# A rational feed-forward after channel attention: cubic and denominator as shifted squares, one way of splitting for every pair, and a branch to the old formulas

## The chip, the cores and the metric

The kernel runs on one core of one Trainium2 chip. The core has TensorE (PE, matmuls; PEld is its weight load), VectorE (DVE), ScalarE (ACT), GpSimd (POOL), SyncE (SP, which issues most DMAs) and 16 DMA engines. The metric is the time of one execution on the device in microseconds; before the change it is 2591.35 (median of 3 runs, 2590.48 to 2592.93). Lower is better.

## The reference

There are 4 batches of 6080 tokens with 256 channels. Attention is over channels: q and k are normalised over the tokens, their 256 x 256 product is put through a softmax, and v is multiplied by it. The result goes through a feed-forward of width 2048 whose activation is a rational function with drawn coefficients a (4) and b (2).

```
qn = q / (norm(q, over tokens) + 1e-6);  kn the same
att = softmax(kn^T @ qn / tau);  x = v @ att          # per batch, 6080 x 256
h = x @ w_in                                          # w_in 256 x 2048 (8 bytes an element)
P = a0 + a1 h + a2 h^2 + a3 h^3
Q = 1 + |b0| |h| + |b1| h^2
out = (P / (Q + 1e-6)) @ w_out                        # w_out 2048 x 256 (8 bytes an element)
```

The inputs are float32, apart from w_in and w_out.

## The kernel before, in words

**Tiling.** The attention matrix of a batch is multiplied into w_in first ("fuse": per pair two tiles w and w2, a high and a low part in float32r). So per group of 512 tokens (the twelfth of a batch has 448) the kernel forms h = v @ w directly, two blocks of 128 hidden units ("a pair") at a time: 8 pairs a group, 12 groups a batch, 384 pairs in all. v is turned on DVE and split into vhi (ACT) and vlo (POOL), both float32r.

**A pair** (function `pair`, lines 824 to 1020): PE makes hx, 128 x 2 x 512 in PSUM, with 12 float32r matmuls (vhi w, vlo w, vhi w2). ACT, DVE and POOL then turn it into g, and PE adds g @ w_out to the accumulator acc (2 banks of PSUM, one buffer). `KIND`, line 52, has four letters for each of the 8 pairs. The first says how g meets w_out: R splits g into gh and gl (both float32r), and PE does 12 float32r matmuls (gh w_out_hi, gh w_out_lo, gl w_out_hi); S keeps g in float32 (in a uu tile), and PE does 4 float32 matmuls with w_out_sb. Four pairs are R, four are S. The second letter says how the denominator is made: F and f by Abs(b1 h), times h plus b0 on DVE, Abs, and plus one (on POOL for F, on ACT for f); U by a square and an Abs on ACT and a product and a sum on POOL. The numerator is always a line a3 h + a2 on ACT ("slope") and two passes on DVE ("num1", "num2"). The reciprocal is Abs_reciprocal_sqrt ("root") and Square on ACT, then one step of correction: "quot" (DVE), "again" (POOL, two halves), "rest" (DVE) and, for R, "last_pool" (POOL), for S "last" (DVE).

**Attention.** Every batch's q and k come in 24 halves of a group into kq tiles; PE adds up their products, ACT squares them, and the squares are added on POOL, on DVE or by an adding DMA. The first batch's halves, 8 pieces of w_in and some of w_out fill the start; the first 10 halves of the second batch ("front") follow.

**Order.** Every step is handed to a `Planner` (lines 120 to 279) with a key: the due time of its pair plus an offset from the table `LAG` (by step name and pair). The planner lists the steps in the order in which a model of the engines would start them, and each engine runs its list in that order. Buffers are rings: three hx, three d, five uu, three r, three gh, two gl, one acc. Line 69 is the helper that issues every instruction, so every row of the profile has that line; rows are told apart by their tiles.

Of the kernel before, what the change touches and what calls it, by code (L numbers as in the profile page):

```python
# [20 lines left out]
LAG = {  # L21
    "first": (-24.0827, 3.1318, 94.51, -24.5032, 22.4371, -51.7071, -86.5307, -21.2765),
    "second": (32.5259, 24.2026, -35.044, 23.3497, 19.1846, -23.3758, 75.5728, 69.5328),
    "line": (-60.3793, -61.2691, -59.8342, -215.9253, -53.1915, -76.184, -176.4998, -1.9601),
    "prod": (-44.6411, -87.224, -31.8158, -156.7696, -54.2751, -78.1687, -52.424, -29.3868),
    "abs": (-34.4285, -122.1588, -58.7602, -98.9991, -109.4362, -197.9928, -178.3656, -100.9785),
    "one": (166.6146, 7.0144, 53.5865, 60.2777, 89.1595, 21.5861, 288.9329, 196.6758),
    "slope": (129.0614, 42.8295, 37.2315, 42.0834, 87.1801, 67.56, 67.4098, -36.9932),
    "num1": (215.3215, 137.6246, 221.5767, 236.6176, 228.2938, 156.502, 166.2629, 171.3395),
    "num2": (153.2124, 60.9084, 12.211, 101.4315, 108.3821, -26.7673, 155.735, 50.8239),  # L30
    "sum": (-114.3088, 29.3047, -115.4251, -167.6125, -59.476, -188.0768, -152.5494, -79.9865),
    "root": (-38.5091, -197.9471, -59.4045, -115.0584, -58.0609, -128.1065, -80.6201, -193.5267),
    "square": (-40.0553, -16.2375, -33.3815, -133.7437, 15.9887, -1.4662, -98.6254, -36.906),
    "quot": (29.4947, -54.9999, -50.3625, -122.0889, -68.6879, -40.3178, -160.6082, -31.8443),
    "again": (-51.7758, -60.2965, -172.0824, -144.6242, -186.8217, -194.2782, -221.1473, -198.5867),
    "rest": (-207.6066, -117.3149, -46.4453, -162.483, -66.4698, -127.5935, -141.4566, -70.1941),
    "last": (-85.0694, -95.1459, 38.415, -140.8617, -144.4619, -72.3023, -75.0525, -34.9464),
    "last_pool": (103.2607, 109.5359, 210.7027, 11.2587, 121.6879, -15.2807, 139.5789, 81.5984),
    "out": (172.8342, 198.8616, 134.7569, 148.4694, 113.0415, 59.72, 9.9512, 73.2606),
    "out_lo": (147.9861, 210.6514, 208.9647, 323.6963, 308.8599, 174.7979, 147.3652, 281.023),  # L40
}
# [241 lines left out]
def tile_channel_attention_rational_ffn(  # L283
# [858 lines left out]
```

## Time and profile before

| | |
|---|---|
| median of the runs | 2591.35 us |
| profiled execution: span | 2590.5 us |
| mean granted clock of TensorE | 0.993 |
| PE busy | 2500.2 us |
| DVE busy | 2379.6 us |
| POOL busy | 2318.0 us |
| ACT busy | 2260.3 us |
| DMA moved | 140.97 MB |

The profiled execution's time is its span, 2590.5 us; the median of the timed runs is 0.9 us above it. Busy times are of one engine; the matmuls of PE are pipelined, so the durations of single matmul records overlap, and the distance between their starts is what one costs. Durations of ACT and DVE records also overlap a little with the next on the same engine.

### The profile page before, as it was taken

To read this page: it belongs to the slowest core of one execution; us is meant where nothing else is said; L and a number is where in the kernel's file an instruction comes from. 1 tells how busy PE (TensorE), PEld (TensorE's weight loads), DVE (VectorE), ACT (ScalarE), POOL (GpSimd) and SP (SyncE) were. 2 spreads that over 40 slices of the span, in tenths; PEclk is the share of its full clock that TensorE was granted. 3 is DMA by queue.
4 is the path that set the end of the run, shared out by engine and by line. 5 is a ranking of instruction groups with operands and counts; after the bars stand their busy time and mean duration, and the time that the engine had idled before them with its cause. 6 is when DMAs were issued, how large, how long until landed. Compare 5 with 4: busy or idle time off the path is not lost.

```text
span 2590.5 us, 29047 instructions
## 1 busy us (share of the span) xinstructions
PE 2500.2 (97%) x9632; PEld 1802.3 (70%) x9632; DVE 2379.6 (92%) x2500; ACT 2260.3 (87%) x2314; POOL 2318.0 (89%) x1725
## 2 busy tenths in 40 slices
PE   8799999999999999999999999999998999999998
PEld 6677666666677776666777776766666667667666
DVE  5889999999888999999978899999997999999997
ACT  5689898898888888988979888898887999999997
POOL 6499999999788999999968999999996999999997
PEclk9899999999999999999999999999999999999999
DMA  9953112102366412112147622112111110110100
GB/s 322 206 126 47 17 17 33 17 16 41 66 153 141 76 17 33 17 17 32 25 90 162 137 39 33 17 17 32 17 17 17 29 20 17 28 22 17 24 9 16
DMA packets 416871, 140.97 MB, mean 54 GB/s; under 512 B 351344, under 2 KB 406064, under 8 KB 416720
## 3 DMA queue, kind: packets, MB, share of 16 engines
q1 hardware_dynamic: 408176, 108.04, 19.4%
q0 software_dynamic: 8544, 31.07, 6.7%
q8 instruction: 76, 1.25, 0.2%
q14 instruction: 75, 0.61, 0.1%
HBM read 83.10 MB, written 24.90 MB: 42 GB/s over the span
## 4 chain that ended last, share of the span: by engine, by line
PE 51%; ACT 15%; POOL 14%; DVE 11%; issue 7%; DMA 3%; SPq 0%; DVEq 0%; POOLq 0%; ACTq 0%
PE hx L69 27%; PE acc L69 24%; POOL d L69 9%; ACT uu L69 6%; ACT r L69 4%; DVE d L69 4%; POOL gl L69 3%; DVE hx L69 3%; ACT d L69 3%; DVE uu L69 2%; POOL vlo L69 1%; DMA kq<-in_k_dram 1%; DVE orow L69 1%; DMA r<-in_q_dram 1%; ACT orow L69 1%
## 5 line engine op out<-in xcount | busy, mean ns | idle before, releaser
L69 PE MATMUL hx<-vhi,w 128*128 128x512 f32 (+1 forms) x3072 | 1082.7, 413 | 11.4 <-DVE uu L69 4.6
L69 PEld LDWEIGHTS hx<-vhi,w 128*128 128x128 f32 x3072 | 580.8, 189 | 192.7 <-DVE d L69 32.3
L69 PE MATMUL acc<-uu,w_out_sb 128*128 128x512 f32 (+1 forms) x1536 | 699.8, 588 | 1.1 <-DVE uu L69 1.1
L69 PE MATMUL hx<-vlo,w 128*128 128x512 f32 (+1 forms) x1536 | 599.7, 390 | 0.0
L69 POOL TENSOR_TENSOR d<-d,gh 128x512 f32<-128x512 f32 (+1 forms) x384 | 485.1, 1290 | 65.7 <-DVE gh L69 53.7
L69 POOL TENSOR_TENSOR d<-d,r 128x512 f32<-128x512 f32 (+1 forms) x384 | 485.5, 1293 | 51.1 <-ACT r L69 49.9
L69 POOL TENSOR_TENSOR gl<-d,r 128x512 fp32r<-128x512 f32 (+1 forms) x384 | 501.2, 1327 | 11.8 <-DVE d L69 11.0
L69 ACT ACTIVATE uu<-hx,babs 128x1024 f32<-128x1024 f32 (+1 forms) x384 | 423.3, 1102 | 83.6 <-PE hx L69 79.4
L69 DVE SCALAR_TENSOR_TENSOR hx<-uu,coef,hx 128x1024 f32<-128x1024 f32 (+1 forms) x384 | 488.8, 1273 | 4.8
L69 DVE TENSOR_TENSOR uu<-uu,hx 128x1024 f32<-128x1024 f32 (+1 forms) x384 | 461.6, 1202 | 30.2 <-ACT uu L69 30.1
L69 PEld LDWEIGHTS acc<-uu,w_out_sb 128*128 128x128 f32 x1536 | 290.1, 189 | 246.4 <-issue 223.2
L69 ACT ACTIVATE uu<-hx,coef 128x1024 f32<-128x1024 f32 (+1 forms) x384 | 458.7, 1195 | 0.1
L69 ACT ACTIVATE r<-d 128x1024 f32<-128x1024 f32 (+1 forms) x384 | 401.9, 1047 | 57.3 <-POOL d L69 53.8
L69 ACT ACTIVATE r<-r 128x1024 f32<-128x1024 f32 (+1 forms) x384 | 401.4, 1047 | 5.0
L69 ACT ACTIVATE d<-d 128x1024 f32<-128x1024 f32 (+1 forms) x336 | 351.1, 1045 | 56.1 <-DVE d L69 55.2
L69 POOL TENSOR_TENSOR d<-d,uu 128x1024 f32<-128x1024 f32 (+1 forms) x144 | 345.9, 2402 | 12.7 <-ACT uu L69 4.6
L69 PEld LDWEIGHTS hx<-vlo,w 128*128 128x128 f32 x1536 | 291.2, 190 | 83.6 <-issue 33.1
L69 DVE SCALAR_TENSOR_TENSOR d<-uu,babs,hx 128x1024 f32<-128x1024 f32 (+1 forms) x240 | 303.6, 1265 | 34.7 <-ACT uu L69 31.1
L69 PE MATMUL acc<-gh,w_out_hi 128*128 128x512 f32 (+1 forms) x768 | 278.1, 443 | 36.7 <-DVE orow L69 25.8
L69 DVE SCALAR_TENSOR_TENSOR d<-hx,coef,d 128x512 f32<-128x512 f32 (+1 forms) x384 | 277.2, 740 | 23.7 <-POOL d L69 23.2
L69 DVE SCALAR_TENSOR_TENSOR uu<-d,hx 128x512 f32<-128x512 f32 (+2 forms) x392 | 256.9, 676 | 16.3 <-POOL d L69 9.1
L69 DVE SCALAR_TENSOR_TENSOR gh<-hx,coef,r 128x1024 fp32r<-128x1024 f32 (+1 forms) x192 | 243.8, 1270 | 22.6 <-ACT r L69 14.9
(99 smaller groups left out, 2831.1 us busy)
## 6 DMA issues: line engine op xcount, KB each, us to landing
ssq<-sq POOLq DMA_DIRECT2D x54, 512.0 KB, 5.0
out_dram<-orow SPq DMA_DIRECT2D x178, 128.0 KB, 3.3
vst<-in_v_dram SPq DMA_DIRECT2D x176, 128.0 KB, 4.0
kq<-in_k_dram SPq DMA_DIRECT2D x78, 256.0 KB, 4.5
kq<-in_q_dram SPq DMA_DIRECT2D x78, 256.0 KB, 4.8
d<-in_moe_w_in_dram SPq DMA_DIRECT2D x8, 512.0 KB, 7.0
ssq<-sq POOLq DMA_DIRECT2D x6, 448.0 KB, 5.3
r<-in_k_dram SPq DMA_DIRECT2D x10, 256.0 KB, 6.5
```

Of the source, the lines that this page charges most:

```text
L69: ins = op(*args, **kwargs)
```

## The change

The numerator is divided by a3 and completed: h^3 + c2 h^2 + c1 h + c0 = h ((h + c2/2)^2 + kappa) + c0. The denominator is divided by |b1|: (|h| + half1)^2 + eps. The factor a3/|b1| ("gain") goes into w_out. So ACT makes the square of the shifted h ("zz"), |h| ("abs"), its shifted square ("shift"), the root of that plus eps and its square; DVE makes h (zz + kappa) ("num") and quot; POOL adds eps to d ("one") and makes "again" in two halves; DVE makes "rest" and "last" in two halves. All 8 pairs are split into gh and gl, so w_out_sb is gone and w_out_hi and w_out_lo hold all of w_out. uu has two buffers and no kk tile. 60 of the squares of q and k go from ACT to POOL. Weight pieces that come late use kq and sq tiles.

36 small operations on DVE at the start compute the constants and a flag, which is 1 where the completed forms do not cancel badly. Then all engines load the flag and branch: one body has the new formulas, the other the old ones (kind F, split R, for every pair). Each body has its own tables and its own plan; `LAG` and `TIME` are new.

```diff
-KIND = ("RfPq", "SUPq", "RFPq", "SUPq", "RfPq", "SUPq", "RFPq", "SFPq")
+LIMIT = 1e6
+SLOT = {"d": 3, "uu": 2, "r": 3, "gh": 3, "gl": 2}
...
-    "line": (-60.3793, -61.2691, -59.8342, -215.9253, -53.1915, -76.184, -176.4998, -1.9601),
+    "shift": (6.5225, -68.5913, -190.892, 31.7758, -179.2847, -141.1578, 314.4052, -28.0943),
...
+    def coefficients():
+
+        t = [test[:, i : i + 1] for i in range(12)]
+        dve.tensor_scalar(t[0], a3, 0.0, None, op0=ALU.is_equal)
+        dve.tensor_tensor(t[1], a3, t[0], op=ALU.add)
+        dve.reciprocal(r3, t[1])
+        dve.tensor_scalar_max(t[2], b1, 1.0 / LIMIT)
+        dve.reciprocal(rb, t[2])
+        dve.tensor_scalar_mul(fast[:, 2:5], coef[:, 0:3], r3)
+        dve.tensor_scalar_mul(half2, c2, 0.5)
+        dve.tensor_tensor(t[3], half2, half2, op=ALU.mult)
+        dve.tensor_tensor(kappa, c1, t[3], op=ALU.subtract)
+        dve.scalar_tensor_tensor(half1, b0, 0.5, rb, op0=ALU.mult, op1=ALU.mult)
+        dve.tensor_scalar_mul(gamma, rb, ONE)
+        dve.tensor_tensor(t[4], half1, half1, op=ALU.mult)
+        dve.tensor_tensor(eps, gamma, t[4], op=ALU.subtract)
+        dve.tensor_tensor(gain, a3, rb, op=ALU.mult)
...
+        dve.scalar_tensor_tensor(t[8], t[6], 64.0, t[7], op0=ALU.mult, op1=ALU.is_ge)
+        dve.scalar_tensor_tensor(t[9], gamma, 4.0, t[4], op0=ALU.mult, op1=ALU.is_ge)
+        dve.tensor_tensor(want, t[8], t[9], op=ALU.mult)
...
+                    if first or i < self.front:
+                        step("ACT", 1.05, at, lambda: act.activation(sq[:pn], src[1](), AF.Square), [kq], [sq])
+                    else:
+                        fn = lambda: pool.tensor_tensor(sq[:pn], src[1](), src[1](), op=ALU.mult)
+                        step("POOL", 2.38, at, fn, [kq], [sq])
...
+            if quick:
+                fn = lambda: act.activation(c(d), c(hx), AF.Abs)
+                put("ACT", 0.87, 0.16, "abs", fn, [hx], [d], 1.0)
+                fn = lambda: act.activation(c(y), c(hx), AF.Square, bias=half2)
+                put("ACT", 0.87, 0.25, "zz", fn, [hx], [y], 1.0)
+                fn = lambda: act.activation(c(d), c(d), AF.Square, bias=half1)
+                put("ACT", 0.87, 0.22, "shift", fn, [d], [d])
+                fn = lambda: dve.scalar_tensor_tensor(c(hx), c(y), kappa, c(hx), op0=ALU.add, op1=ALU.mult)
+                put("DVE", 1.06, 0.23, "num", fn, [y, hx], [hx])
+                fn = lambda: act.activation(c(r), c(d), AF.Abs_reciprocal_sqrt, bias=eps)
+                put("ACT", 0.87, 0.22, "root", fn, [d], [r], 6.0)
+                fn = lambda: pool.tensor_scalar(c(d), c(d), ones[:, 0:1], eps, op0=ALU.mult, op1=ALU.add)
+                put("POOL", 1.06, 0.1, "one", fn, [d], [d])
+                first = c0
...
+                fn = lambda: dve.scalar_tensor_tensor(
+                    hx[:, x, :n], hx[:, x, :n], first, d[:, x, :n], op0=ALU.add, op1=ALU.subtract
+                )
+                put("DVE", 0.53, 0.22, "rest", fn, [h, d, t_ok[x]], [h], later=0.1 * x)
+                fn = lambda: dve.tensor_tensor(glo[:, x, :n], hx[:, x, :n], r[:, x, :n], op=ALU.mult)
+                put("DVE", 0.53, 0.14, "last", fn, [h, r, *([glo] if x else [])], [glo_ok[x], *([] if x else [glo])], 10.0, 0.1 * x)
...
+    way = nc.values_load(flag[0:1, 0:1], min_val=0, max_val=1)
+    with tc.If(way > 0) as branch:
+        for s in plans[0]:
+            s.fn()
+    seen.clear()
+    with branch.Else():
+        for s in plans[1]:
+            s.fn()
```

At the start, the queue of SP before the change reads like this (coef holds a, b and tau; kq holds halves of k and q):

```order
L69 DMA coef_71<-in_moe_a_dram 128x4
L69 DMA coef_71<-in_moe_b_dram 128x2
L69 DMA coef_71<-in_tau_dram 128x1
L69 DMA kq0_95<-in_k_dram 128x2x256
L69 DMA kq0_95<-in_q_dram 128x2x256
L69 DMA kq1_96<-in_k_dram 128x2x256
```

And after it (flag is the result of the 36 operations on DVE):

```order
L79 DMA coef_71<-in_moe_a_dram 128x4
L79 DMA coef_71<-in_moe_b_dram 128x2
L79 DMA coef_71<-in_tau_dram 128x1
L1044 TENSOR_LOAD flag_83
L1045 COMPARE_AND_BRANCH
L79 DMA d0_123<-in_moe_w_in_dram 128x1024
L79 DMA kq0_132<-in_k_dram 128x2x256
L79 DMA kq0_132<-in_q_dram 128x2x256
```

The load of the flag and the branch stand ahead of the first load of data; the same two rows stand at the head of PE, DVE, ACT and POOL.

On PE, before the first softmax, the kernel before has these rows (hx0 ends the first batch's scores, acc0 takes the front halves of the second, ones and orow make the norms):

```order
L69 MATMUL hx0_142<-r2_105 128x256 x4
L69 MATMUL acc0_94<-kq0_95 128x256 x4
L69 MATMUL acc0_94<-kq1_96 128x256 x4
L69 MATMUL acc0_94<-kq2_97 128x256 x4
L69 MATMUL acc0_94<-kq3_98 128x256 x4
L69 MATMUL acc0_94<-kq0_95 128x256 x4
L69 MATMUL acc0_94<-kq1_96 128x256 x4
L69 MATMUL acc0_94<-kq2_97 128x256 x4
L69 MATMUL hx2_144<-ones_69,orow0_99 128x1 x4
```

The changed kernel has these at the same place:

```order
L79 MATMUL hx0_176<-r1_130 128x256 x4
L79 MATMUL acc0_128<-kq0_132 128x256 x4
L79 MATMUL hx1_177<-ones_69,orow0_138 128x1 x4
L79 MATMUL hx1_177<-kq1_133,ones_69 128x128 x2
L79 MATMUL hx0_176<-ident_64,kq2_134 128x128 x4
```

Six of the seven front halves that stood ahead of the norms now stand behind them, among the first pairs.

In the last batch, PE's second products of an R pair and an S pair before (the names gh, gl: the split g; uu: g in float32; hx: the first product of another pair, of which the first rows stand):

```order
L69 MATMUL acc0_94<-gh1_138,w_out_hi_84 128x512 x2
L69 MATMUL acc0_94<-gh1_138,w_out_lo_85 128x512 x2
L69 MATMUL acc0_94<-gl0_140,w_out_hi_84 128x512 x2
L69 MATMUL acc0_94<-uu2_91,w_out_sb_83 128x512 x2
L69 MATMUL hx2_144<-vhi1_132,w1_115 128x512
L69 MATMUL hx2_144<-vlo1_134,w1_115 128x512
L69 MATMUL hx2_144<-vhi1_132,w21_123 128x512
```

And at such a place after:

```order
L79 MATMUL acc0_128<-gh0_171,w_out_hi_121 128x512 x2
L79 MATMUL acc0_128<-gh0_171,w_out_lo_122 128x512 x2
L79 MATMUL hx0_176<-vhi1_166,w1_149 128x512
L79 MATMUL hx0_176<-vlo1_168,w1_149 128x512
L79 MATMUL hx0_176<-vhi1_166,w21_157 128x512
L79 MATMUL acc0_128<-gl1_175,w_out_hi_121 128x512 x2
```

Every pair's second product is now in float32r, with half a first product of a later pair between gh and gl.

## Rows read from the trace of the kernel before

**Rows 1.** The page: busy us, share of the span, instructions.
```profile
PE 2500.2 (97%) x9632; PEld 1802.3 (70%) x9632; DVE 2379.6 (92%) x2500; ACT 2260.3 (87%) x2314; POOL 2318.0 (89%) x1725
```
**Rows 2.** Stages: stretch, length, busy PE PEld DVE ACT POOL, clock, DMA share, GB/s.
```profile
0.00:60.00 60.00, 48.03 (x203) 40.16 (x204) 33.75 (x48) 32.98 (x36) 41.01 (x24) 1.00 1.01 325
60.00:120.00 60.00, 49.76 (x202) 40.59 (x202) 50.97 (x84) 35.56 (x55) 28.58 (x14) 0.86 0.87 212
...
2250.00:2500.00 250.00, 246.17 (x945) 173.29 (x945) 239.08 (x238) 233.69 (x232) 238.53 (x177) 1.00 0.10 19
```
**Rows 3.** Timeline of ACT (start, us, what): the accumulator read at two groups' ends.
```profile
2402.34 1.00 ACT L69 COPY orow<-acc 128x1024 f32<-128x1024 f32 x1
...
2450.93 1.00 ACT L69 COPY orow<-acc 128x1024 f32<-128x1024 f32 x1
```
**Rows 4.** Waits of PE, 240 to 2500 us: total us, times, longest.
```profile
PE acc L69 <- DVE orow L69: 25.8, 13, 2.3
```
**Rows 5.** Timeline of PE: starts of an R set, an S set, the next R.
```profile
1520.52 0.62 PE L69 MATMUL acc<-gh,w_out_hi 128*128 128x512 f32 x2
...
1523.25 3.59 PE L69 MATMUL acc<-uu,w_out_sb 128*128 128x512 f32 x8
...
1527.14 0.63 PE L69 MATMUL acc<-gh,w_out_lo 128*128 128x512 f32 x2
```
**Rows 6.** Groups of instructions on ACT: busy us, mean ns, idle before.
```profile
L69 ACT ACTIVATE uu<-hx,coef 128x1024 f32<-128x1024 f32 (+1 forms) x384 | 458.7, 1195 | 0.1
L69 ACT ACTIVATE uu<-hx,babs 128x1024 f32<-128x1024 f32 (+1 forms) x384 | 423.3, 1102 | 83.6 <-PE hx L69 79.4 <-PE acc L69 1.9 <-DVE d L69 0.4
...
L69 ACT ACTIVATE r<-d 128x1024 f32<-128x1024 f32 (+1 forms) x384 | 401.9, 1047 | 57.3 <-POOL d L69 53.8
...
L69 ACT ACTIVATE d<-d 128x1024 f32<-128x1024 f32 (+1 forms) x336 | 351.1, 1045 | 56.1 <-DVE d L69 55.2 <-POOL gl L69 0.9
...
L69 ACT ACTIVATE d<-hx 128x1024 f32<-128x1024 f32 (+1 forms) x144 | 145.1, 1007 | 29.1 <-PE hx L69 28.2 <-issue 0.5
```
**Rows 7.** Groups on DVE: num2, num1, the denominator, rest, the old last, quot.
```profile
L69 DVE SCALAR_TENSOR_TENSOR hx<-uu,coef,hx 128x1024 f32<-128x1024 f32 (+1 forms) x384 | 488.8, 1273 | 4.8
...
L69 DVE TENSOR_TENSOR uu<-uu,hx 128x1024 f32<-128x1024 f32 (+1 forms) x384 | 461.6, 1202 | 30.2 <-ACT uu L69 30.1
...
L69 DVE SCALAR_TENSOR_TENSOR d<-uu,babs,hx 128x1024 f32<-128x1024 f32 (+1 forms) x240 | 303.6, 1265 | 34.7 <-ACT uu L69 31.1 <-issue 1.2
...
L69 DVE SCALAR_TENSOR_TENSOR d<-hx,coef,d 128x512 f32<-128x512 f32 (+1 forms) x384 | 277.2, 740 | 23.7 <-POOL d L69 23.2
L69 DVE SCALAR_TENSOR_TENSOR uu<-d,hx 128x512 f32<-128x512 f32 (+2 forms) x392 | 256.9, 676 | 16.3 <-POOL d L69 9.1 <-DVE hx L69 0.5
...
L69 DVE SCALAR_TENSOR_TENSOR gh<-hx,coef,r 128x1024 fp32r<-128x1024 f32 (+1 forms) x192 | 243.8, 1270 | 22.6 <-ACT r L69 14.9
```
**Rows 8.** Groups on POOL: the old last of R, U's sum, F's plus one.
```profile
L69 POOL TENSOR_TENSOR gl<-d,r 128x512 fp32r<-128x512 f32 (+1 forms) x384 | 501.2, 1327 | 11.8 <-DVE d L69 11.0 <-ACT r L69 0.8
...
L69 POOL TENSOR_TENSOR d<-d,uu 128x1024 f32<-128x1024 f32 (+1 forms) x144 | 345.9, 2402 | 12.7 <-ACT uu L69 4.6
...
L69 POOL TENSOR_SCALAR d<-d,ones 128x1024 f32<-128x1024 f32 (+1 forms) x144 | 166.1, 1153 | 5.7 <-ACT r L69 5.5
```
**Rows 9.** Timeline of the start: tau and k issued, tau used, first pair's product.
```profile
1.67 0.43 SPq L69 DMA_DIRECT2D coef<-in_tau_dram  x1
2.14 0.43 SPq L69 DMA_DIRECT2D kq<-in_k_dram  x1
...
4.67 0.16 DVE L69 RECIPROCAL rtau<-coef 128x1 f32<-128x1 f32 x1 [4.67 <-DMA coef<-in_tau_dram]
...
111.92 0.58 PE L69 MATMUL hx<-vhi,w 128*128 128x512 f32 x1
```
**Rows 10.** Timeline of DVE: small operations in a chain.
```profile
83.08 0.16 DVE L69 SCALAR_TENSOR_TENSOR e<-e,s 128x4 f32<-128x4 f32 x1
83.28 0.16 DVE L69 SCALAR_TENSOR_TENSOR e<-y,e 128x4 f32<-128x4 f32 x1
```

More of the change, by code (lines that the diff above doesn't have):

```diff
@@ new lines @@
+    "attn0_0": 45.8526, "attn_0": 1.1865, "attn0": -6.3363, "attn": 0.9219, "attn1": 89.2338,
+    "value": 15.6212, "fuse": -17.2442, "back": 41.3761, "store": 342.9423, "finish": 48.2092,
+    "front": 84.9867, "front_pace": 31.406, "ahead_pe": 1000000000.0, "ahead_act": 1000000000.0,
+    "ahead_dve": 1000000000.0, "ahead_pool": 1000000000.0,
+}
+GENERAL_LAG = {
+    "mm1": 0.0, "kk": 3.0, "prod": 4.2, "slope": 4.1, "num1": 5.4, "absd": 5.5, "num2": 6.7, "root": 6.6,
+    "one": 7.6, "square": 7.7, "quot": 8.8, "again": 10.1, "rest": 12.3, "last": 13.8, "out": 14.3, "out_lo": 17.3,
+}
@@ L771, in values @@
[L771 to L781 removed]
+    fast = const.tile([P, 12], F32, name="fast")
+    r3, rb, c0, c1, c2, half2, kappa, half1, gamma, eps, gain, want = (fast[:, i : i + 1] for i in range(12))
@@ new lines, in body @@
+        for n, (side, m) in enumerate(EARLY):
+            c = when["in0"] + when["in"] * n if side == "in" else when["early"] + when["early_pace"] * m
+            piece(side, m, c - 6.0, c)
+        late = [("out", m, when["out0"] + when["out"] * m) for m in range(NFP) if ("out", m) not in EARLY]
+        for n, (side, m, c) in enumerate(sorted(late, key=lambda x: x[2])):
+            piece(side, m, T0 + c - 6.0, T0 + c)
+        attns = [Attn(0, 0.0, when["load"], when["softmax"])]
+        vparts = [values(0, when["softmax"])]
@@ new lines, in body @@
+        gate = [attns[0].w[0][0]]
+        for G in range(TG):
+            b, g = divmod(G, NG)
+            at = T0 + G * NFP * II
+            if g == 0 and b + 1 < B:
+                attns.append(None)
+                begin, pace = ("attn0", "attn") if b else ("attn0_0", "attn_0")
+                attns[b + 1] = Attn(b + 1, at + when[begin] * II, when[pace] * II, at + when["attn1"] * II)
+            if G + 1 < TG:
+                vparts.append(values(G + 1, at + when["value"] * II, gate if G == 0 else ()))
+            acc = buf("acc", [P, NC2, GT])
+            for p in range(NFP):
+                pair(G * NFP + p, at + p * II, vparts[G], attns[b].w[p], acc)
+            finish(G, at + NFP * II + when["finish"], acc)
@@ new lines, in body @@
+        return plan.order()
+    plans = [body(True), body(False)]
+    homes["hx"] = 2 * GT
+    for tag, width in homes.items():
+        if tag in ("hA", "hB"):
+            continue
+        home, n = (ps, SLOTS["hA" if tag == "hx" else tag]) if tag in ("hx", "acc") else (sb, SLOTS[tag])
+        homes[tag] = [home.tile([P, width], F32, name=f"{tag}{i}") for i in range(n)]
+    way = nc.values_load(flag[0:1, 0:1], min_val=0, max_val=1)
+    with tc.If(way > 0) as branch:
+        for s in plans[0]:
+            s.fn()
```

1068 lines of the change are left out of this document (459 added, 609 removed).

## The prediction

> **What bounds the kernel now.** I read the engines' shares first, then the table by stage, then the pitch of one group, then the waits, then single operations. Over the span PE is busy 97%, DVE 92%, POOL 89%, ACT 87% [rows 1]: no engine is far behind. By stage [rows 2], the first two minutes of the table (0 to 120 us) are the start, where the DMA engines are full and PE is busy for 97.8 of 120 us. In a late stretch without attention work PE is busy 246.2 of 250 us, DVE 239.1, POOL 238.5, ACT 233.7. There one group of 512 tokens (8 pairs) takes 2450.93 - 2402.34 = 48.6 us [rows 3]. PE's own need for it, with the prices worked out below, is 8 x 2.73 for the first products, 4 x 2.73 and 4 x 3.435 for the second, and about 1 for the transposes at the group's end: 47.5 us. So PE sets the pace with 1 us of air, and DVE, POOL and ACT follow within 3 to 5 us. Of what PE waits for, the largest single entry is the one accumulator, which DVE must empty between groups: 25.8 us in 13 waits [rows 4]. I take PE as the bound and the other three as the next bounds, which matters because the change moves work on all four.
>
> **PE's second product.** All of it is matmuls into acc. For a pair of kind R it is 12 matmuls in float32r: from 1520.52 to 1523.25, 2.73 us. For a pair of kind S it is 4 matmuls in float32 (8 records): from 1523.25 to 1527.14 lie one S set and the first two matmuls of the next R set (2 x 2.73 / 12 = 0.455), so 3.435 us [rows 5]. The change turns S into R: 0.705 us less for each of 4 x 48 = 192 pairs. A batch has 11 groups of 512 and one of 448 tokens, mean 506.7, so the saving is 0.705 x 192 x 506.7 / 512 = 134 us. No other product changes. Since PE is the bound and its rows stand without gaps, all of it lies on the path, if nothing else becomes late.
>
> In the Trainium skill, page Perfetto Trace Analysis, section Identifying the Most-Contended Engine, matmul busy time is called a poor measure of how full PE is, and the share of weight loads is to be used. By that rule PE would be 70% full [rows 1], DVE with 92% the bound, and the saving on PE worth nothing by itself; the sum would then follow DVE's saving below. The rows speak against it: starts 0.2275 us apart through a whole set [rows 5], and the long float32 passes alone pull the share of weight loads down.
>
> **ACT.** Removed: the slope (458.7 us), the scaled Abs (423.3), 336 passes d<-d (351.1) and 144 passes d<-hx (145.1) [rows 6]: 1378 us. Added for each of 384 pairs: Abs of hx at 1.007, a Square of hx with one column operand as bias at 1.102 (the price of the row with one such operand), a Square d<-d at 1.045 or, if the column operand costs there what it does between the rows 1.007, 1.102 and 1.195, at 1.14; the root (1.047) also gets a column operand, 0 to 0.094 more. 60 squares of k and q move to POOL, 63 us at 1.045. Net -230 to -157 us: ACT 2030 to 2103 us. I take the middle, 2067.
>
> **DVE.** Per pair now: num 1.273, quot 1.270, two times rest 0.740, two times last. The new last (hx times r, 512 columns, hx in PSUM) has no row; its bounds are half of the full-width product (1.202 / 2 = 0.60) and the row of rest, 0.740; I take 0.67, near the 0.676 of the old last [rows 7]. The sum is 488.8 + 487.6 + 554.4 + 514.6 = 2045 us. Before: 488.8 + 461.6 + 303.6 + 277.2 + 256.9 and two quots of 243.8 = 2276. Net -231 (-285 to -177): DVE about 2149 us.
>
> **POOL.** Removed: gl (501.2) and d<-d,uu (345.9), and 144 passes of d by b1 plus one, at the price of the ones row, 166. Added: the pass by ones for 240 more pairs (277), 60 squares at 2.402 (144) [rows 8]. The product "again" stays, 768 times. Net -592: POOL about 1726 us.
>
> So with 2590.5 - 134 = 2456 us the shares would be PE 96%, DVE 87%, ACT 84%, POOL 70%. The three that could have taken PE's place all fall by at least as much in share as PE does. The buffers kept are those that the ring of a pair needs: from its first product to the last read of its hx go 2.73 (PE), 5.3 (five ACT passes, which now stand in a row), 1.27 (quot), 2.58 (again, both halves), 0.74 (rest), and six handovers, some 13.3 us; three slots of hx at a pitch of 6 us give 18. The uu tile lives only from zz to num, so two slots cover it.
>
> **The start.** Before, SP issued the first load of k at 2.14 us [rows 9]. Now every engine waits for the flag, and what is queued behind it is the whole program: SP's loads, PE's first product. The flag needs 36 operations on DVE, each on what the one before wrote; small ones in a chain start 0.20 us apart (83.08, 83.28 [rows 10]). They begin when tau is there and its two operations are done, 4.67 + 2 x 0.20 = 5.1, and end at 12.3 us. Reading the flag into a register has no row: between nothing and the 3.0 us that the load of tau took from its issue at 1.67 to its use at 4.67 [rows 9]; I take 1. The start moves by 13.3 - 2.1 = 11 us (10 to 13). On the other side, PE's order puts the norms of the first softmax behind one half of the next batch's scores, where it was behind seven (each waits for two loads); the other halves now come later, between pairs. PE is idle 22 of the first 120 us [rows 2], so part of the 11 us can be filled: from nothing to all. I take 5 back: +6 net (0 to +13).
>
> In the Trainium skill, page Runtime: NRT & Kernel Launch, section Instruction fetch mechanics, a taken branch whose target is not in the window has to fetch its code first. Here the branch at the end of the quick body jumps over the whole old one. Without that rule the jump costs nothing in the sum; with it, one transfer more, 3.0 us by the row of tau [rows 9], and the time below would be 3 us longer. No run so far shows it.
>
> **The sum.** 2590.5 - 134 + 6 = 2462.5; the median of the runs is 0.9 us above the span, so 2463. The waits in the steady part I leave as they are, though less load on DVE should shorten some: I take 2 us for it and write 2461.
>
> **Rivals.**
> 1. The saving turns into new waits. The low part gl came from POOL for R pairs and now comes from DVE, behind rest and in line with the next pair's num; PE's gl products stand in order behind it. For: DVE does rest and last twice per pair now, in between two POOL passes. Against: DVE falls to 87%. At 0.17 us a pair, a quarter of one last, 384 pairs lose 65 us: 2526.
> 2. More than the sum. DVE is what PE waited for most, 25.8 us at acc and a few at hx [rows 4], and DVE falls by 231 us. If half of the waits and the whole start shift vanish: 2461 - 15 - 6 = 2440, and down to 2425 if the pairs of the first group start sooner too.
> 3. Slower: the ring. hx has three slots as before, but ACT's five passes of a pair stand in a row, so a pair that comes just behind another waits up to 5.4 us, and then up to 2.5 us for DVE. From 13.3 the ring grows to 21 us, a pitch of 7.0 instead of 6. It decides where the ring is over 3 x 6.4 = 19 us. Then 384 x (7.0 - 6.0) = 384 us more than forecast at most; at 20 us, 2461 + 384 x 0.67 = 2718. Against: it needs ACT full, and ACT is at 84%.
> 4. The change does not do what it says: the flag is 0 and the old formulas run. Then DVE does eight passes a pair, 1.265 + 1.202 + 1.273 + 1.270 + 1.48 + 1.34 = 7.83 us [rows 7], 3007 us in all, and with its other work (2379.6 - 2276 = 104) over 3110. For the drawn coefficients (a 0.505, -0.235, -0.287, 0.280; |b| 3.21, 3.90) the two conditions hold by far: 129 against 0.07, and 1.03 against 0.17.
>
> **Chances.** The forecast with its own range 2445 to 2485: 0.67. Rival 1: 0.15. Rival 2: 0.12. Rival 3: 0.03. Rival 4: 0.02. No change to measure: 0.01. The range 2425 to 2520 holds the forecast, rival 2 and half of rival 1. A measurement of this kernel tells 0.2%, about 5 us, from no change: faster 0.94, within 0.01, slower 0.05.
>
> **What would show it.** Right: no float32 record with acc as target; a group of the last batch in 48.6 - 2.8 = 45.8 us; PE 96% busy, DVE and ACT under 90%, POOL near 70%; the first load of k at about 13 us. Wrong: PE waiting often for gl or hx, or a pitch over 46.5 us in the last batch (rivals 1 and 3); a first product of a pair before the 111.92 us of now [rows 9] (rival 2); slope passes by coef in the trace (rival 4).

## The result, and the profile after

The changed kernel takes 2477.77 us (median of 4 runs, 2477.43 to 2478.46), the kernel before on the same chip 2592.14: a ratio of 0.9559, 95% interval 0.9545 to 0.9572, 114 us less. The forecast was 2461, the range 2425 to 2520. The profiled execution took 2477.43 us, its span is 2475.4.

The page, against [rows 1]:

```profile
PE 2375.3 (96%) x10400; PEld 1942.0 (78%) x10400; DVE 2196.5 (89%) x2684; ACT 2169.3 (88%) x2156; POOL 1770.5 (72%) x1353
```

The stages, against [rows 2] (stretch, length, busy PE PEld DVE ACT POOL, clock, DMA share, GB/s):

```profile
0.00:60.00 60.00, 33.25 (x136) 28.08 (x136) 39.42 (x72) 23.77 (x26) 30.94 (x19) 0.94 0.82 246
60.00:120.00 60.00, 40.76 (x164) 34.58 (x165) 47.25 (x91) 31.75 (x51) 17.25 (x7) 0.77 0.48 143
...
2250.00:2475.00 225.00, 210.17 (x944) 171.76 (x942) 193.06 (x230) 199.88 (x199) 147.10 (x117) 0.99 0.11 22
```

The start holds less: PE is busy 74 of the first 120 us instead of 97.8. The pitch (the distance from one group to the next) in the last batch, on ACT, against [rows 3], is 46.17 us where 45.8 was forecast:

```profile
2060.12 1.00 ACT L79 COPY orow<-acc 128x1024 f32<-128x1024 f32 x1
...
2106.29 0.99 ACT L79 COPY orow<-acc 128x1024 f32<-128x1024 f32 x1
```

Waits of PE from 240 us to the end (total us, times, longest), against [rows 4]; DVE's orow isn't waited for any more, and the wait for a slot of hx, which gl's pass frees, stands first (before, PE waited 5.9 us for DVE's uu and 4.1 for its d at hx):

```profile
PE hx L79 <- DVE gl L79: 27.6, 41, 3.4
...
PE acc L79 <- DVE gl L79: 2.4, 2, 1.6
```

One set on PE, against [rows 5]: every second product is float32r, and 1520.24 to 1522.96 is 2.72 us a set, the old price.

```profile
1520.24 0.62 PE L79 MATMUL acc<-gh,w_out_hi 128*128 128x512 f32 x2
...
1521.15 0.62 PE L79 MATMUL acc<-gl,w_out_hi 128*128 128x512 f32 x2
...
1522.96 0.39 PE L79 MATMUL hx<-vhi,w 128*128 128x512 f32 x1
```

Groups of ACT (root and shift, each with a column operand), against [rows 6]:

```profile
L79 ACT ACTIVATE r<-d,fast 128x1024 f32<-128x1024 f32 (+1 forms) x384 | 439.7, 1145 | 10.9
L79 ACT ACTIVATE d<-d,fast 128x1024 f32<-128x1024 f32 (+1 forms) x384 | 439.4, 1145 | 8.5
```

Groups of DVE (rest, last, num, quot), against [rows 7]; the two transposes of a group, of v and of acc, took 1.22 and 1.23 us each:

```profile
L79 DVE SCALAR_TENSOR_TENSOR hx<-hx,fast,d 128x512 f32<-128x512 f32 (+1 forms) x768 | 574.7, 748 | 82.3 <-POOL d L79 53.4
L79 DVE TENSOR_TENSOR gl<-hx,r 128x512 fp32r<-128x512 f32 (+1 forms) x768 | 516.9, 681 | 40.3 <-PE acc L79 3.2 <-DVE hx L79 0.9
L79 DVE SCALAR_TENSOR_TENSOR hx<-uu,fast,hx 128x1024 f32<-128x1024 f32 (+1 forms) x384 | 487.2, 1269 | 45.3 <-ACT d L79 35.6 <-ACT uu L79 8.1 <-PE hx L79 1.4
L79 DVE SCALAR_TENSOR_TENSOR gh<-hx,fast,r 128x1024 fp32r<-128x1024 f32 (+1 forms) x384 | 485.8, 1265 | 42.1 <-ACT r L79 34.8 <-PE acc L79 6.8
```

POOL's pass by one, against [rows 8]:

```profile
L79 POOL TENSOR_SCALAR d<-d,ones,fast 128x1024 f32<-128x1024 f32 (+1 forms) x384 | 470.7, 1226 | 101.0 <-ACT r L79 100.6
```

The start, against [rows 9] (the first load of data at 11.22, with the flag done at 10.56, and the first pair's product at 117.08 instead of 111.92):

```profile
11.22 0.33 SPq L79 DMA_DIRECT2D d<-in_moe_w_in_dram  x1
...
117.08 0.58 PE L79 MATMUL hx<-vhi,w 128*128 128x512 f32 x1
```

DVE's reads of acc mark the groups' ends; here are those that end the first three batches, of the kernel before and of the changed one:

```profile
757.87 1.10 DVE L69 STREAM_TRANSPOSE orow<-acc 128x896 f32<-128x896 f32 x1
1390.15 1.11 DVE L69 STREAM_TRANSPOSE orow<-acc 128x896 f32<-128x896 f32 x1
2011.24 1.11 DVE L69 STREAM_TRANSPOSE orow<-acc 128x896 f32<-128x896 f32 x1
```

```profile
740.97 1.12 DVE L79 STREAM_TRANSPOSE orow<-acc 128x896 f32<-128x896 f32 x1
...
1335.11 1.12 DVE L79 STREAM_TRANSPOSE orow<-acc 128x896 f32<-128x896 f32 x1 [0.35 <-PE acc L79]
...
1914.93 1.12 DVE L79 STREAM_TRANSPOSE orow<-acc 128x896 f32<-128x896 f32 x1 [1.44 <-PE acc L79]
```

So the four batches, the last one up to the span's end, give 16.9, 38.1, 41.3 and 18.8 us, where PE's saving alone would be 33.5 each. In the middle of each of the first three batches a group now takes 45.0 us throughout, from one read of acc to the next:

```profile
993.27 1.25 DVE L79 STREAM_TRANSPOSE orow<-acc 128x1024 f32<-128x1024 f32 x1
...
1038.24 1.24 DVE L79 STREAM_TRANSPOSE orow<-acc 128x1024 f32<-128x1024 f32 x1
```

Before, groups of 43 to 52 us took turns in the middle of the second and the third batch (here 51.7, the one ahead of it 43.1), 48.5 us on average, and the first batch had groups of 47 to 50:

```profile
1067.51 1.24 DVE L69 STREAM_TRANSPOSE orow<-acc 128x1024 f32<-128x1024 f32 x1
...
1119.19 1.24 DVE L69 STREAM_TRANSPOSE orow<-acc 128x1024 f32<-128x1024 f32 x1
```

### The profile page after: what moved, and what is told of

Its sections match the earlier page's. It is cut to its first block, busy times and chain, and to the rows that moved or that the text cites. A ratio compares the mean times of both kernels' runs of the same rounds, so it can differ in the third digit from the quotient of the medians.

```text
span 2475.4 us, 30913 instructions
## 1 busy us (share of the span) xinstructions
PE 2375.3 (96%) x10400; PEld 1942.0 (78%) x10400; DVE 2196.5 (89%) x2684; ACT 2169.3 (88%) x2156; POOL 1770.5 (72%) x1353
## 4 chain that ended last, share of the span: by engine, by line
PE 74%; DVE 12%; issue 5%; ACT 3%; POOL 2%; DMA 2%; SPq 1%; DVEq 0%; POOLq 0%; ACTq 0%
PE hx L79 40%; PE acc L79 34%; DVE hx L79 5%; DVE gl L79 4%; DVE gh L79 2%; POOL d L79 1%; SPq L79 1%; ACT d L79 1%; ACT r L79 1%; DMA kq<-in_q_dram 1%; DVE orow L79 1%; ACT uu L79 1%; DMA d<-in_moe_w_in_dram 1%; ACT L79 0%; DMA r<-in_k_dram 0%
## 5 line engine op out<-in xcount | busy, mean ns | idle before, releaser
L79 POOL TENSOR_TENSOR d<-d,gh 128x512 f32<-128x512 f32 (+1 forms) x768 | 977.9, 1304 | 498.0 <-DVE gh L79 495.2
L79 PE MATMUL hx<-vhi,w 128*128 128x512 f32 (+1 forms) x3072 | 1046.1, 395 | 30.0 <-DVE gl L79 27.6
L79 DVE SCALAR_TENSOR_TENSOR hx<-hx,fast,d 128x512 f32<-128x512 f32 (+1 forms) x768 | 574.7, 748 | 82.3 <-POOL d L79 53.4
L79 DVE TENSOR_TENSOR gl<-hx,r 128x512 fp32r<-128x512 f32 (+1 forms) x768 | 516.9, 681 | 40.3 <-PE acc L79 3.2
L79 POOL TENSOR_SCALAR d<-d,ones,fast 128x1024 f32<-128x1024 f32 (+1 forms) x384 | 470.7, 1226 | 101.0 <-ACT r L79 100.6
L79 DVE SCALAR_TENSOR_TENSOR hx<-uu,fast,hx 128x1024 f32<-128x1024 f32 (+1 forms) x384 | 487.2, 1269 | 45.3 <-ACT d L79 35.6
L79 DVE SCALAR_TENSOR_TENSOR gh<-hx,fast,r 128x1024 fp32r<-128x1024 f32 (+1 forms) x384 | 485.8, 1265 | 42.1 <-ACT r L79 34.8
L79 PE MATMUL acc<-gl,w_out_hi 128*128 128x512 f32 (+1 forms) x1536 | 473.8, 390 | 4.4 <-DVE gl L79 4.3
L79 PE MATMUL acc<-gh,w_out_lo 128*128 128x512 f32 (+1 forms) x1536 | 470.3, 387 | 0.0
L79 ACT ACTIVATE r<-d,fast 128x1024 f32<-128x1024 f32 (+1 forms) x384 | 439.7, 1145 | 10.9
L79 ACT ACTIVATE d<-d,fast 128x1024 f32<-128x1024 f32 (+1 forms) x384 | 439.4, 1145 | 8.5
```

The costliest lines, as they stand in the source:

```text
L79: ins = op(*args, **kwargs)
```

## The experiments

Times are medians; each is compared with 2477.8. Runs of one kernel lie up to 6.6 us apart, so a difference of 5 us or less is not shown by the time alone; there the text says what the trace shows.

**1. Half of the pairs back in float32.**

```diff
+            def one_f32(x):
+                for e in range(NC2):
+                    pe.matmul(
+                        acc[:, e, :n], w_out_hi[:, 2 * p + x, e * P : (e + 1) * P].bitcast(F32),
+                        ghi[:, x, :n].bitcast(F32), start=False, stop=(end and x == 1),
+                    )
...
             def out_hi(x):
...
+                if quick and p % 2:
+                    fn = lambda: one_f32(x)
...
             def out_lo(x):
...
+                if quick and p % 2:
+                    fn = lambda: None
```

> The second product of four of eight pairs (the odd ones) is four float32 matmuls with w_out_hi again, as before the change; gl of these pairs is still made but no product reads it, and w_out_lo is left out for them. All other work and the order are those after the change. Theory A (PE's second product is what the change saves): 0.705 us more for each of 192 pairs, +134 us, about 2612, which is 20 us above the kernel before. Rival B (a part of the saving came from elsewhere, and PE has slack that the other engines leave): +100 us or less, 2578 or less.

Measured: 2555.83 us, ratio to before 0.9855 (0.9840 to 0.9870): +78, not +134. Theory A fell, rival B came. The stretch 900 to 1080 us of this kernel, and then of the changed one:

```profile
900.00:1080.00 180.00, 180.00 (x678) 127.27 (x677) 168.94 (x194) 167.60 (x160) 124.07 (x97) 1.00 0.15 24
```

```profile
900.00:1080.00 180.00, 177.52 (x768) 142.88 (x767) 171.82 (x201) 173.24 (x165) 129.36 (x101) 1.00 0.15 24
```

The price of a float32 set is the predicted one: between these starts of the variant lie half a set and two products of hx, so a set takes 2 x (1517.24 - 1515.06 - 2 x 0.2275) = 3.45 us.

```profile
1515.06 0.39 PE L79 MATMUL hx<-vhi,w 128*128 128x512 f32 x1
1515.29 1.88 PE L79 MATMUL acc<-gh,w_out_hi 128*128 128x512 f32 x4
1516.61 0.79 PE L79 MATMUL hx<-vhi,w 128*128 128x512 f32 x1
1517.24 0.40 PE L79 MATMUL hx<-vlo,w 128*128 128x512 f32 x1
```

With the float32 products PE has no gap at all in this stretch and a group takes 46.5 us (1021.01 to 1067.56, by the reads of acc); that is PE's own need. Less 4 x 0.705 it would be 43.7, but the changed kernel takes 45.0. So the price of the second product was right and 56 of its 134 us didn't arrive, since something else sets 45.0. And with PE's need as before the change (46.5 a group), the kernel is still 38 us faster than the one before (2593.78 in these runs): that much the rest of the change gives. The trace agrees: from 240 us on, all of PE's waits add up to 58 us in the kernel before and to 12 in this one. Whether the lighter DVE, ACT and POOL or the new tables of the plan took them away was not tested apart. Its batches end here:

```profile
760.26 1.12 DVE L79 STREAM_TRANSPOSE orow<-acc 128x896 f32<-128x896 f32 x1 [1.30 <-PE acc L79]
...
1374.65 1.12 DVE L79 STREAM_TRANSPOSE orow<-acc 128x896 f32<-128x896 f32 x1 [1.50 <-PE acc L79]
...
1975.06 1.12 DVE L79 STREAM_TRANSPOSE orow<-acc 128x896 f32<-128x896 f32 x1 [2.02 <-PE acc L79]
```

Against the kernel before, its batches differ by +2.4, -17.9, -20.7 and -2.2 us (span 2552.1); from it to the changed kernel it is -19.3, -20.3, -20.6 and -16.6. So the second products give an even 17 to 21 a batch instead of 33.5, and the rest of the change pays in the second and third batch alone. That fits the start, whose work of PE moves into the first batch (PE was busy 97.8 us of the first 120 before, 74 after the change).

**2. What sets 45.0: PE's products of gl, and ACT's column operands.** First gl is still made, but no product reads it.

```diff
-                fn = lambda: mm2((w_out_hi,), (glo,), [x], False, end)
+                fn = lambda: None
```

> PE leaves out the products of gl (gl is still made), 0.91 us less for each of 384 pairs, so PE's own need of a group falls from 43.7 to 36.4 us. Theory A (after the change DVE, ACT and the ring of hx already set the pace nearly as tightly as PE): a group goes from 45.0 to no less than 43.3 us, which is ACT's busy time in it, and the time falls by 20 to 80 us only, to 2400 or more. Rival B (PE alone is the bound): the time falls by most of 0.91 x 384 = 349 us, to 2200 or less.

Measured: 2444.38 us, -33. A group takes 44.4 to 44.5 although PE now needs 36.4: PE is not the bound of the middle groups, as theory A has it.

Then the shift loses its bias and the root adds a constant, so this kernel computes another function.

```diff
-                fn = lambda: act.activation(c(d), c(d), AF.Square, bias=half1)
+                fn = lambda: act.activation(c(d), c(d), AF.Square)
...
-                fn = lambda: act.activation(c(r), c(d), AF.Abs_reciprocal_sqrt, bias=eps)
+                fn = lambda: act.activation(c(r), c(d), AF.Abs_reciprocal_sqrt, bias=ONE)
```

> The shift is a Square without a bias and the root adds a constant instead of the column eps, so the output is another function; order and plan are the same. Theory A (in the last batch ACT, 96% busy in 2000 to 2250 us, is the bound beside PE, and its two column operands cost 0.098 us each): ACT's busy time falls by 2 x 0.098 x 384 = 75 us to about 2094, the pitch of a group of the last batch falls from 46.1 to about 45.5, and the time by 10 to 20 us, to about 2463. Rival B (PE alone is the bound, ACT's share costs nothing): ACT falls by the same 75 us and the time by less than 4 us.

Measured: 2469.51 us, -8.3, between theory A's 10 to 20 and rival B's 4. ACT's busy time fell by 61 us to 2108.7, the middle groups went from 45.0 to 44.9, those of the last batch from 46.1 to 45.8. ACT is not the bound of the middle groups either.

**3. DVE.** Its timeline in the changed kernel, one pair and a half (start, us, operation):

```profile
963.21 1.27 DVE L79 SCALAR_TENSOR_TENSOR gh<-hx,fast,r 128x1024 fp32r<-128x1024 f32 x1
964.40 0.68 DVE L79 TENSOR_TENSOR gl<-hx,r 128x512 fp32r<-128x512 f32 x1
965.00 1.28 DVE L79 SCALAR_TENSOR_TENSOR hx<-uu,fast,hx 128x1024 f32<-128x1024 f32 x1
966.19 0.75 DVE L79 SCALAR_TENSOR_TENSOR hx<-hx,fast,d 128x512 f32<-128x512 f32 x1
967.04 0.69 DVE L79 TENSOR_TENSOR gl<-hx,r 128x512 fp32r<-128x512 f32 x1
967.84 0.76 DVE L79 SCALAR_TENSOR_TENSOR hx<-hx,fast,d 128x512 f32<-128x512 f32 x1
968.51 1.27 DVE L79 SCALAR_TENSOR_TENSOR gh<-hx,fast,r 128x1024 fp32r<-128x1024 f32 x1
```

No row here names a releaser, that is, an engine for which DVE waits; in the six groups from 948 us on only two passes a group wait, 0.29 us each, for POOL. Most passes overlap the one before by some 0.08 us, but gl starts 0.10 us behind the end of the rest that it reads, and the next rest 0.11 behind that gl. A pair takes 968.51 - 963.21 = 5.30 us; eight of them and two transposes are nearly the whole 45.0. The page's 89% hides it, since it is a mean with stages in which DVE has less to do. In the kernel without gl's products the same rest and gl stand closer, 0.03 us apart instead of 0.10 (there gl has no product of PE to wait for):

```profile
966.37 0.76 DVE L79 SCALAR_TENSOR_TENSOR hx<-hx,fast,d 128x512 f32<-128x512 f32 x1
967.16 0.69 DVE L79 TENSOR_TENSOR gl<-hx,r 128x512 fp32r<-128x512 f32 x1
```

Eight such places a group give 0.56 us, about what that kernel gained a group, while PE's need had fallen by 7.3. The test takes load from DVE (half of each gl is left as it was) and keeps the order of every engine:

```diff
-                fn = lambda: dve.tensor_tensor(glo[:, x, :n], hx[:, x, :n], r[:, x, :n], op=ALU.mult)
+                u = n // 2 if quick and m >= NFP else n
+                fn = lambda: dve.tensor_tensor(glo[:, x, :u], hx[:, x, :u], r[:, x, :u], op=ALU.mult)
```

> From the second group on, last makes only half of the columns of gl (256 of 512; the rest of gl is left as it was), so DVE loses 16 x 0.27 = 4.3 us a group; the order of all engines is word for word that after the change. A pair takes DVE 5.30 us from one gh to the next, without idle; 8 of these and two transposes of 1.17 are 44.7 of the 45.0 us of a group. Theory A (DVE sets the pace in the first three batches): the pitch there falls from 45.0 to PE's own 43.7, at most 44.0, the last batch's by less (46.1 to 45.5 or so), and the time by 45 to 65 us, to 2413 to 2433. Rival B (ACT, 43.3 us busy of 45.0, sets it, DVE only follows): the pitch stays above 44.6 and the time falls by less than 20 us.

Measured: 2424.26 us, -53.5 (ratio to before 0.9349, 0.9335 to 0.9364). Middle groups take 43.6, those of the last batch 44.8 (45.5 expected), and PE has no gap in the middle groups. Theory A holds.

```profile
1019.24 1.24 DVE L79 STREAM_TRANSPOSE orow<-acc 128x1024 f32<-128x1024 f32 x1
...
1062.85 1.24 DVE L79 STREAM_TRANSPOSE orow<-acc 128x1024 f32<-128x1024 f32 x1
```

```profile
900.00:1080.00 180.00, 180.00 (x794) 148.39 (x793) 163.88 (x208) 177.19 (x170) 133.96 (x105) 1.00 0.15 24
```

> As the kernel with last on half of the columns, and besides the shift without a bias and the root with a constant (another function; ACT loses 1.2 to 1.6 us a group). Theory A (DVE sets the pace in the first three batches, and ACT in the last): in the first three batches the pitch is PE's 43.7 with or without the constants, within 0.2 us; in the last batch it falls from 46.1 to 44.7 to 45.0, which is PE's own; the time is 10 to 20 us under that of half of last alone. Rival B (the last batch waits for something else, the chain of acc, its copy and its transposes): its pitch stays above 45.4.

The edits are those of the two kernels above together. Measured: 2413.80 us, 10.5 less than with half of last alone (4.2 of it by the end of the first batch). Middle groups take 43.5, those of the last batch 44.7.

So PE's own need is 43.5 and 44.7, and the changed kernel pays 1.5 and 1.4 a group above it. Theory A is borne out in the first three batches. In the last one its ACT is not: relief of DVE alone had brought 46.1 to 44.8, relief of ACT alone only to 45.8. Nor is DVE full there: in seven groups from 2060 us on it waits 7.9 us for POOL's d and 6.3 for ACT's r. Which step sets the pitch of the last batch stays open.

**4. Two ways to relieve DVE that keep the result.** One releases hx earlier, the other gives last of two pairs to POOL.

```diff
...
-                    hx[:, x, :n], hx[:, x, :n], first, d[:, x, :n], op0=ALU.add, op1=ALU.subtract
+                    d[:, x, :n], hx[:, x, :n], first, d[:, x, :n], op0=ALU.add, op1=ALU.subtract
...
-                fn = lambda: dve.tensor_tensor(glo[:, x, :n], hx[:, x, :n], r[:, x, :n], op=ALU.mult)
+                fn = lambda: dve.tensor_tensor(glo[:, x, :n], d[:, x, :n], r[:, x, :n], op=ALU.mult)
```

> The step rest writes into d (SBUF) instead of hx (PSUM), and last multiplies d by r; so hx is free for PE one DVE pass (0.68 us) and its place in the queue earlier, nothing else changes. In the steady part a group takes 45.0 us (last batch 46.1), while the float32 variant showed PE's own need: 46.5 less 4 x 0.705 is 43.7 (last batch 44.7). Theory A (the missing 1.3 us a group are PE waiting for a free hx, which last holds): the pitch falls to 43.9 to 44.4, the time by 30 to 50 us, to 2430 to 2450. Rival B (a DVE pass with all operands in SBUF is slowed beside POOL, as the weight pieces in the start, 0.917 and 1.452 us instead of 0.69): last takes 0.9 us or more, DVE grows by 170 us or more and becomes the bound, the time is 2530 or more.

Measured: 2880.74 us, +403. Rival B's price came (last 0.910 us with both operands in SBUF, instead of 0.681), and POOL's pass by one was slower too (1.450 in the same stretch, instead of 1.226). DVE's group from 1000 to 1180 us:

```profile
L79 DVE TENSOR_TENSOR gl<-d,r 128x512 fp32r<-128x512 f32 x53 | 47.1, 910 | 0.6
```

That agrees with the Trainium skill, page GPSIMD Engine Reference, section Key points: GpSimd shares its SBUF interfaces with VectorE, and instructions of VectorE with two SBUF inputs contend with it. In the trace a single gl took 1.02 us beside POOL's pass by one (at 1016.85) and 0.64 with POOL idle (at 1018.96). But DVE's 229 us more don't make 403, and no engine was the bound: PE 87%, DVE 84%. A part goes with TensorE's clock: its granted mean fell from 0.987 to 0.954 while PE waited more, and PE was busy 127 us longer with as many matmuls.

```diff
+AWAY = (1, 5)
...
+                away = quick and p in AWAY
+                left, left_ok = (d, u_ok[x]) if away else (hx, h)
...
-                fn = lambda: dve.tensor_tensor(glo[:, x, :n], hx[:, x, :n], r[:, x, :n], op=ALU.mult)
...
+                e, name, per, fixed = (pool, "POOL", 1.16, 0.14) if away else (dve, "DVE", 0.53, 0.14)
+                fn = lambda: e.tensor_tensor(glo[:, x, :n], left[:, x, :n], r[:, x, :n], op=ALU.mult)
```

> In two of eight pairs (1 and 5) rest writes into d and POOL makes last (gl from d and r), as the R pairs did before the change: DVE loses 2 x 2 x 0.68 = 2.7 us a group, POOL gains 2 x 2 x 1.33 = 5.3 us (it is busy 32.3 of 45.0), and hx of these pairs is free earlier. The results stay the same. Theory A (DVE, through the slot of hx that it frees last, costs PE 1.3 us a group): the pitch falls by 0.4 to 1.0 us and the time by 15 to 45 us, to 2435 to 2463. Rival B (ACT, 96% busy, holds the pitch by itself): no change beyond 5 us. Rival C (gl comes later, POOL being slower, and PE waits for it at acc): PE's waits for gl grow and the time with them, 2485 or more.

Measured: 2777.35 us, +300. Theory A and rival B fell. Rival C has the sign, but not the cause: PE's waits at acc for gl grew only from 2.4 to 25 us. Its page:

```profile
PE 2454.2 (88%) x10400; PEld 1994.4 (72%) x10400; DVE 2098.4 (76%) x2492; ACT 2141.8 (77%) x2156; POOL 1998.9 (72%) x1545
```

DVE did get lighter, by 98 us, yet every engine idles, and groups take from 42.7 to over 54 us. Here too the granted clock fell, to 0.950, and PE was busy 79 us longer. Both kernels hold d longer than the plan's tables assume, and in both the planner listed the steps in another order, which the kernels of the third experiment did not. That the order is the cause fits, but wasn't taken apart (with the order after the change, d would be overwritten too early), so the cause of the 403 and the 300 us stays open.

**5. The start and the exit.**

```diff
-    way = nc.values_load(flag[0:1, 0:1], min_val=0, max_val=1)
-    with tc.If(way > 0) as branch:
-        for s in plans[0]:
-            s.fn()
...
+    for s in plans[0]:
+        s.fn()
```

> Only the body with the new formulas is in the program: no load of the flag, no branch, no old body; the 36 small operations on DVE stay. Order and plan of that body are the same. Theory A (the flag and the branch hold up the start): the first load of k and q is issued at about 2 us instead of 11.6, the first pair's product starts near 108 us instead of 117, and the whole is 8 to 10 us shorter, about 2469; of this about 1 us is time outside the span (2.0 us with the branch, 0.9 before the change). Rival B (the start is bound by what comes behind the loads, the weight pieces on DVE and the norms): the loads start at 2 us all the same, but the first pair moves by 3 us or less and the time is 2474 or more.

Measured: 2469.78 us, -8.0. The loads start at 2.13 us and PE's first product at 9.48 instead of 17.79, but the first pair only at 115.11 instead of 117.08, and the first group ends 3.4 us earlier. Theory A has the sum, but not the place: the first pair moves by 2 us only, as rival B has it, and half of the gain lies at the end. Here are the last stores of the changed kernel and of this one; their spans end at 2475.4 and 2466.0, so 6.7 and 2.7 us behind the end of the issue.

```profile
2466.90 1.78 SPq L79 DMA_DIRECT2D out_dram<-orow  x4
```

```profile
2461.56 1.78 SPq L79 DMA_DIRECT2D out_dram<-orow  x4
```

```diff
-    with tc.If(way > 0) as branch:
+    with tc.If(way > 0):
         for s in plans[0]:
-            s.fn()
-    seen.clear()
-    with branch.Else():
-        for s in plans[1]:
             s.fn()
```

> The flag is loaded and all engines branch as after the change, but the old body is not in the program, so the branch at the end of the new one jumps over nothing. Without any branch the end came 2.7 us after the last store was issued, after the change 6.7. Theory A (the jump over the old body costs the 4 us): the end comes 2.7 to 3.5 us after the last store, the start is as after the change (first load at about 11 us), time 2473 to 2475. Rival B (the engines' meeting at the end of the branch costs it, whatever lies behind): 6 to 7 us again, time within 1.5 us of 2477.8.

Measured: 2473.37 us, -4.4. The first load is at 11.24, as after the change, and the span of 2468.0 ends 2.8 us behind the last store, issued here:

```profile
2463.45 1.78 SPq L79 DMA_DIRECT2D out_dram<-orow  x4
```

Theory A: the jump over the old body is the 4 us. The trace shows the fetch that the prediction names: in the last 16 us of the changed kernel the DMA queues of the kind "instruction" moved 12 packets, in the last 16 us of this kernel one.

```profile
q14 instruction: 9, 0.07, 1.6%
q8 instruction: 3, 0.05, 1.4%
```

```profile
q8 instruction: 1, 0.02, 0.4%
```

The jump costs 4 us here, against the 3.0 that the prediction took from a row.

```diff
+    ahead, taken = [], set()
+    for s in plans[0]:
+        fresh = all(b.tag is None or (b.tag, b.slot) not in taken for b in s.bufs)
+        if s.eng == "SP" and s.new and fresh and not s.waits:
+            s.fn()
+            ahead.append(s)
...
     way = nc.values_load(flag[0:1, 0:1], min_val=0, max_val=1)
```

> The first 12 loads of the new body (two pieces of w_in, five halves of k and q) are issued by SP ahead of the load of the flag and the branch; all else is the same, the old body included. Without any branch the first group ended 3.4 us earlier and the last 5.3 us earlier, and the end after the last store came 4.1 us sooner. Theory A (in the start it is the loads that the flag holds up, and the exit of the branch is a cost by itself): the start comes back, the exit stays; 3 to 6 us less than after the change, 2472 to 2475. Rival B (the engines' own wait at the branch costs the start, the loads don't matter): within 1.5 us of 2478.

Measured: 2474.85 us (2473.51 to 2476.52), -2.9. PE's first product is at 12.38, where the flag ends its wait. Theory A, as far as the trace goes: the first group ends 1.4 us earlier (194.08 against 195.47), and the exit stays. Whether the kernel is faster than the changed one is not shown: the ratios to the kernel before, 0.9543 (0.9530 to 0.9556) and 0.9559 (0.9545 to 0.9572), overlap.

```diff
-    with tc.If(way > 0) as branch:
-        for s in plans[0]:
+    with tc.If(way < 1) as branch:
+        for s in plans[1]:
...
     with branch.Else():
-        for s in plans[1]:
+        for s in plans[0]:
```

> Two edits of what is around the bodies, none inside them: 11 loads (two of w_in, the rest halves of k and q) go out ahead of the branch, and the old body stands first, the new one behind it, so that the jump over the old body happens at the start and the new body runs out at the end of the program. Theory A (the start is held up by its loads, the exit costs 4 us by the jump over the old body, and at the start the same jump is hidden while the first loads are in flight): the end comes 2.7 us after the last store instead of 6.7, and the time is 2.9 us (loads ahead alone) and 4.1 us less than 2477.8: 2469 to 2473. Rival B (the jump costs its 4 us wherever it stands): 2473 to 2476, with PE's first product 3 us or more later than the 12.4 us of the loads ahead alone.

Measured: 2477.09 us, no gain. The span ends 2.9 us behind the end of the last store's issue instead of 6.7. But at the start ACT goes on at 16.18 instead of 12.15, 4.0 us later than with the loads ahead alone, and PE's first product is at 18.52 instead of 12.38; from 11 to 19 us the DMA queues of the kind "instruction" move 9 packets there, and none with the loads ahead alone. The jump costs where it stands. Rival B in kind, 1 us worse in size.

```diff
-    "front": 84.9867, "front_pace": 31.406, ...
+    "front": 84.9867, "front_pace": 1.9188, ...
```

> One number of the plan's table is changed: the distance of the front halves of the second batch goes from 31.4 to 1.9 us, so nearly all ten stand ahead of the norms on PE, as before the change. Theory A (batch 0 lost 16.6 us against PE's saving, because PE idles in the start and does these halves later, between pairs): PE is busier in 0 to 120 us by up to 9 x 1.75 = 16 us and the whole is 5 to 12 us shorter, about 2469. Rival B (the start is bound by its loads and by DVE): each half needs two loads more ahead of the first softmax, the norms and the first pair come 5 to 13 us later, what PE gains there is lost again, and the time is within 4 us of 2478 or longer.

Measured: 2493.65 us, +15.9. The first group ends at 213.71 instead of 195.47, and only 1.7 of these 18.2 us come back in the first batch (757.51 against 740.97). PE is no busier in the first 120 us (73.2 against 74.0). Rival B: the front halves cost the same or more ahead of the softmax.

## Why the prediction was right, point by point

**The sum.** 2461 was 17 us low, but two of its terms were each off by more, in opposite senses: 56 us of PE's saving did not arrive, and some 46 came from waits that the sum put at 2. That they nearly cancel is luck; the range held for that reason, and not because both terms were right.

**PE's second product, -134.** The price holds (3.45 us a float32 set by the pitch, 2.72 a float32r set), and it was the largest term; what failed is the sentence that all of it lies on the path. Undone alone it is worth 78 us, because behind it DVE's own need of a group sets the pace in the first three batches. That could have been read before: by its rows [rows 7] DVE needs 8 x (1.273 + 1.270 + 2 x 0.740 + 2 x 0.67) = 42.9 us a group and two transposes more, some 45, against 47.5 - 2.8 = 44.7 for PE. I compared shares of the span, and my one stage was the last batch, where DVE turns no acc.

**Waits, -2.** They were worth far more: with PE's work as before, the rest of the change gives 38 us net, and the flag and the branch cost 8 of it (2477.8 to 2469.8), so some 46 by estimate; PE's waits fell by as much, from 58 us to 12. I looked for waits in the last batch, where PE had 1 us of air a group, but most lie in the first three. There a middle group took 48.5 us on average in the second and third, and PE's need was 46.5.

**Rival 1 (new waits for gl, 2526)** named the right place, a last pass in line with num, but not its form: PE waits for gl at acc for 2.4 us only. It waits for hx, which gl's pass frees (27.6 us in 41 waits), one of the signs of being wrong that I had named. The ring that I added up ended with rest and left out last, which reads hx behind it. It came together with rival 2, more than the sum: both were half true, and the forecast between them held.

**The weight-load rule.** It would have made the saving worth nothing by itself and DVE the bound. The runs lie between: DVE is the next bound, and 78 of 134 us arrived. But PE without a gap shows 127.27 of 180 us of weight loads, 71%, in the float32 variant: a low share didn't mean room.

**The start, +6.** The flag moved it much as forecast (first load 11.2 instead of 13.3, since many of the 36 operations start 0.07 us apart and not 0.20), and the first pair comes 5.2 us later. But by the end of the first group only 0.7 us of it is left in the float32 variant (197.06 against 196.40), and without any branch 3.4 us more are gained there. What the sum left out is the exit, 4.1 us; I had named it, at 3.0, but put it at nothing.

**Around the span, +0.9.** No change: the runs of the kernel before beside the experiments lie 1.8 us above their spans, those after 2.0. The jump's 4.1 us are inside the span.

**ACT, DVE, POOL.** The sum of ACT's durations fell by 157 us (2428.0 to 2270.6), the upper end of what I gave: a column operand costs 0.098 in shift and root alike. Its busy time fell by only 91, because records overlap by 101 us now and by 168 before. DVE fell by 183 (177 to 285 given), POOL by 548 (592).

**Rivals 3 and 4** did not come: the new body ran, and with the order as planned the ring of hx did not grow.

## What to carry to other kernels

Before calling one engine the bound, add up every engine's need for one unit of the repeated work, in each stage that differs: shares of the span average over stages, and an engine at 89% can set the pace. To learn what one edit of several is worth, undo it alone: the parts of a change need not add up, since relief of a second engine pays only until the first is full, and the reverse. An order written for one set of lifetimes is part of the kernel; a relief that leaves it word for word gave what was expected, two that did not lost 300 us and more, though how much of that is the order's stays open.

## What the runs showed of the hardware that was not expected

The jump over a whole body costs 4.1 us at the end of the program, and at the start 4.0 us on ACT (12.15 to 16.18) and 6.1 on PE (12.38 to 18.52); the queues of the kind "instruction" moved packets at just these places, 12 at the end and 9 at the start. A DVE product of 512 columns took 0.681 us with one operand in PSUM and 0.910 with both in SBUF beside POOL's passes, and those grew with it, 1.226 to 1.450. On DVE gl starts 0.10 us after the end of the rest that it reads (967.04), but 0.03 after it where no product of PE reads gl (967.16 in the kernel without gl's products); num, which reads nothing of the gl ahead of it, starts 0.08 us before that gl's end (965.00).
